# Fewer, longer attention stretches between the dense matmuls of a retention and feed-forward kernel

## The chip, the core and the metric

The kernel runs on one core of a Trainium2 chip. Its engines are TensorE (PE, matrix products; PEld is its weight load), VectorE (DVE), ScalarE (ACT), GpSimd (POOL) and SyncE (SP, which here only issues transfers). Each works through its own queue in program order and waits for the others by semaphores. PE writes its results to PSUM, where the kernel's tiles take eight banks; everything else lies in SBUF. The metric is the device time of one launch in microseconds, lower is better.

## What is computed

Causal retention over 8 batches, 8 heads, 576 tokens, head size 64, and then a feed-forward layer with a snake-like activation:

```python
scores = scale * np.matmul(q, k.transpose(0, 1, 3, 2))
Dmat = np.where(rel >= 0, gamma[:, None, None] ** rel[None, :, :], 0.0)
attn = np.matmul(scores * Dmat[None, :, :, :], v)
x = np.ascontiguousarray(attn.transpose(0, 2, 1, 3)).reshape(B * S, H * D)   # 4608 x 512
h = x @ w_in                       # 512 -> 2048
s = np.sin(alpha * h)
g = h + s * s / (alpha + 1e-09)
out = g @ w_out                    # 2048 -> 512
```

## The kernel before

**Tiling.** The 4608 rows of `x` are nine blocks of 512. Block `b` (0 to 7) holds the first 512 tokens of batch `b`; block 8 holds the last 64 tokens of all eight batches. The decay factors are folded into the casts of `q` and `k` to 16 bit, so a score needs only a causal mask (0 or 1). The first 512 tokens of a batch are two halves `p` of 256 tokens, and each half is two chunks `g` of 128. Inside a chunk scores are masked and multiplied with `v`; what earlier chunks contribute comes through a state: `outer` computes `kv` per chunk, `chain` on POOL fades and adds it up (lines 353 to 360), and `states` multiplies it with `q`.

**Steps of one batch** (class `Attention`):
- `cast_half`: half of the heads of `k` or `q` of one `p`, multiplied with the factors (128x512), on DVE for batches 5 to 7. Four of them per `p`, eight per batch.
- `crossed(p)`: two transposes by DMA, `kT` and `qT`, issued by SP.
- `scores(p, y)`: 64x64 matmuls for two of four pairs of heads, `a = 2y` and `2y + 1`, into one tile `sc` of two PSUM banks, and a DVE instruction that multiplies the mask in and writes `ret` in 16 bit. In batches 4 to 7 (`split(b)`) keys of a chunk come as an early half (`r = 0`), which all 128 tokens of the chunk may see, and a late half (`r = 1`), which only the last 64 tokens may see; so each `sc` holds, for each `a`, 128 columns and 64 columns, 192 of 256 used (lines 366 to 399).
- `outer((0, 1))`: 64 matmuls of 64x64 into `kv`, then ACT copies `kv` to `kvs`, and POOL's chain follows.
- `values(p)`: 64x64 matmuls of `ret` and `v` into `o`; `states(p)`: 128x128 matmuls into the same `o` (4 for `p = 0`, 8 for `p = 1`); `take_x(p)`: copies `o` to `x` in 16 bit. `add_states` is `states` and `take_x` on ACT.

The last 64 tokens of four batches at a time are class `Rest`: `scores` (32 matmuls of 64x64, a mask on DVE) and `values` (32 of 64x64, 16 of 128x64 with the states, two copies by ACT).

**Order.** It is written out by hand. A table (lines 588 to 928) covers the start and blocks 0 and 1; it isn't changed. Then a loop over blocks `n = 2 ... 8` runs 16 units `u` each: `gemm1(n, u)` (four matmuls of 128x512 into a bank `hps`, and the sine on ACT), then whatever `at_unit(u, ...)` has put there, then the square on ACT, the product on DVE (`gT`, line 560) and a quarter of `gemm2` of the block before (four matmuls of 128x512). Every fourth quarter ends a PSUM tile `ops`, which ACT copies out and SP sends. In units 1, 5, 9 and 13 the quarter comes before the square and the product.

While block `n` is computed, attention runs for batch `n + 1` (`A`), and batch `n + 2` is cast and transposed (`A2`); its raw `q` and `k` were loaded from unit 12 of the block before. `CASTS[n]` names the units of the eight casts. `crossed(0)` follows one unit after the fourth, `crossed(1)` one after the eighth. So PE switches from dense matmuls to attention and back in units 0, 2, 7 and 10 of each block 3 to 6. In block 5 it does so also in units 12 and 14, for `Rest` of batches 0 to 3; `Rest` of batches 4 to 7 stands in units 0 and 2 of block 7.

**Buffers.** PSUM: tag "mm" is two tiles of two banks (for `sc`, `kv`, `o`), "hp" three banks (for `hps`), "op" one bank (`ops`). SBUF: `ret` has 4 buffers, `kT` and `qT` 3, `v` 6, raw loads 6, `osb` 4.

Of the kernel before, what the change touches and what calls it, by code (L numbers as in the profile page):

```python
# [9 lines left out]
F32 = mybir.dt.float32  # L10
F16 = mybir.dt.float16
ADD = mybir.AluOpType.add
MULT = mybir.AluOpType.mult
# [3 lines left out]
def kernel(  # L17
# [10 lines left out]
    nc = tc.nc  # L28
# [4 lines left out]
    P = 128  # L33
# [44 lines left out]
    work = ctx.enter_context(tc.tile_pool(name="w", bufs=1))  # L78
    psum = ctx.enter_context(tc.tile_pool(name="p", bufs=1, space=bass.MemoryType.PSUM))
# [6 lines left out]
    two = const.tile([P, 192], F16, tag="two", bufs=1)  # L86
# [23 lines left out]
    half = {}  # L110

    def split(b):
        return b >= 4
# [7 lines left out]
    def load_v(b, p):  # L121
        t_ = work.tile([P, H, 2, D], F16, tag="v16", bufs=6, name="v16")
        half[b, "v", p] = t_
        if split(b):
            for g, s, xs in pieces(b, p):
                nc.gpsimd.dma_start(t_[halves(g), :, s], v[b, :, xs, :].rearrange("h i d -> i h d"))  # L126
            return None
        i_ = nc.gpsimd.dma_start(
            t_.rearrange("p h r d -> p h (r d)"),
            v[b, :, 256 * p : 256 * p + 256, :].rearrange("h (i r) d -> i h (r d)", r=2),  # L130
        )
        half[b, "v", p] = t_
        return i_

    def load_rest_v(G):
        t_ = work.tile([P, 2 * H, D], F16, tag="vr16", bufs=1, name="v16")
        for e in range(2):
            b = 4 * G + 2 * e
            nc.gpsimd.dma_start(t_[halves(e)], v[b : b + 2, :, 512:576, :].rearrange("b h i d -> i (b h) d"))
        half[G, "v", "rest"] = t_  # L140

    def load(b, nm, p):
        t_ = work.tile([P, H, 2 * D], F32, tag="raw", bufs=6, name=nm + "32")
        raw[b, nm, p] = t_
        if split(b) and nm == "k":
            for g, s, xs in pieces(b, p):
                nc.sync.dma_start(
                    t_[halves(g), :, 64 * s : 64 * s + 64], src[nm][b, :, xs, :].rearrange("h i d -> i h d")
                )
            return None  # L150
        return nc.sync.dma_start(t_, src[nm][b, :, 256 * p : 256 * p + 256, :].rearrange("h (i r) d -> i h (r d)", r=2))
# [13 lines left out]
    def load_rest(G, nm):  # L165
        t_ = work.tile([P, H, 2 * D], F32, tag="raw", bufs=6, name=nm + "32")
        for e in range(2):
            b = 4 * G + 2 * e
            nc.sync.dma_start(
                t_[halves(e)].rearrange("p h (x d) -> p (h x) d", d=D),  # L170
                src[nm][b : b + 2, :, 512:576, :].rearrange("b h i d -> i (b h) d"),
            )
        raw[G, nm, "rest"] = t_
# [29 lines left out]
    def cast_half(b, nm, p, t, eng):  # L203
        if (b, nm, p) not in half:
            half[b, nm, p] = work.tile([P, 4, 2, 2, D], F16, tag=nm + "16", bufs=nbuf[nm], name=nm + "16")
        if eng is nc.scalar:
            for y in range(4):
                for r in range(2):
                    h = head_of(y, t)
                    eng.mul(  # L210
                        half[b, nm, p][:, y, r, t, :], raw[b, nm, p][:, h, D * r : D * r + D],
                        fac[nm][:, 2 * h + r : 2 * h + r + 1],
                    )
            return
        eng.tensor_tensor(  # L215
            half[b, nm, p][:, :, :, t, :],
            raw[b, nm, p].rearrange("p (a t) (r d) -> p a t r d", t=2, r=2)[:, :, t],
            (ct if nm == "k" and split(b) else fac[nm]).rearrange("p (a t r) -> p a t r", a=4, t=2)[:, :, t].unsqueeze(3).to_broadcast([P, 4, 2, D]),
            MULT,
        )  # L220

    def halves(n):
        return slice(64 * n, 64 * n + 64)

    def head_of(a, t):
        return 2 * a + t
# [17 lines left out]
    class Attention:  # L244
# [144 lines left out]
        def scores_mask(self, p, y):  # L389
            sc = self.sc.pop((p, y))  # L390
            ret = work.tile([P, 2, 512], F16, tag="ret", bufs=4, name="ret")
            n, m_ = (192, two) if split(self.b) else (256, mask[:, 0:256])
            nc.vector.tensor_tensor(  # L393
                ret.rearrange("p t (z x) -> p (t z) x", z=2)[:, :, 0:n],
                sc.rearrange("p t (z x) -> p (t z) x", z=2)[:, :, 0:n],
                m_.unsqueeze(1).to_broadcast([P, 4, n]),
                MULT,
            )
            self.ret[p, y] = ret

        def new_o(self, p, *tags):
            if tags:
                o = [psum.tile([P, 512], F32, tag=t, bufs=3 if t == "hp" else 1, name="o") for t in tags]
            else:
                o = psum.tile([P, 2, 512], F32, tag="mm", bufs=2, name="o")
                o = [o[:, 0], o[:, 1], o]
            self.o[p] = o, set()
# [118 lines left out]
    def gemm1(n, fc, o=None):  # L526
        gemm1_pe(n, fc, o)
        sine(n, fc)
# [403 lines left out]
    V, A_, G_ = nc.vector, nc.scalar, nc.gpsimd  # L932

    with tc.manual_schedule():
# [34 lines left out]
        def of(b):  # L969
            if b not in att:  # L970
                att[b] = Attention(b)
            return att[b]
# [130 lines left out]
        rest = [Rest(0), Rest(1)]  # L1103
        nc.sync.dma_start(two, two_dram.ap())
        nc.sync.dma_start(ct, ct_dram.ap())
        for p, nm in HALVES:
            load(4, nm, p)
        CASTS = (), (), (5, 5, 6, 6, 7, 8, 9, 9), (4, 5, 6, 6, 8, 9, 10, 10), *[(1, 3, 4, 5, 6, 8, 9, 10)] * 2
        for n in range(2, NBLK):
            A = A2  # L1110
            todo = {}

            def at_unit(u, *fs):
                todo.setdefault(u, []).extend(fs)

            if A:
                if n == 2:
                    at_unit(1, lambda: A.scores(0, 0), lambda: A.scores(0, 1))
                    at_unit(4, lambda: A.outer((0, 1)), lambda: A.chain((0, 1, 2, 3)), lambda: A.scores(1, 0))
                else:  # L1120
                    at_unit(0, lambda: A.scores(0, 0), lambda: A.scores(0, 1))
                    at_unit(2, lambda: A.outer((0, 1)), lambda: A.chain((0, 1, 2, 3)), lambda: A.scores(1, 0))
                at_unit(7, lambda: A.scores(1, 1), lambda: A.values(0), lambda: A.add_states(0))
                at_unit(10, lambda: A.values(1), lambda: A.add_states(1))
            bn = n + 2
            if bn < B:
                A2 = of(bn)
                at_unit(0, lambda: load_v(bn, 0), lambda: load_v(bn, 1))
                for i, u in enumerate(CASTS[n]):
                    p, nm, t = i // 4, "kq"[i // 2 % 2], i % 2  # L1130
                    at_unit(u, lambda p=p, nm=nm, t=t: cast_half(bn, nm, p, t, V if n > 2 else G_))
                at_unit(CASTS[n][3] + 1, lambda: A2.crossed(0))
                at_unit(CASTS[n][7] + 1, lambda: A2.crossed(1))
            else:
                A2 = None
            if bn + 1 < B:
                for i, (p, nm) in enumerate(HALVES):
                    at_unit(i + 12, lambda nm=nm, p=p: load(bn + 1, nm, p))
            if n in (3, 5):
                at_unit(15, *[lambda nm=nm: load_rest((n - 3) // 2, nm) for nm in "kq"])  # L1140
                at_unit(15, lambda: load_rest_v((n - 3) // 2))
            R = rest[(n - 4) // 2] if n in (4, 6) else None
            if n in (4, 6):
                at_unit(11 if n == 4 else 5, lambda: cast((n - 4) // 2, "k", "rest", V))
                at_unit(13 if n == 4 else 8, lambda: cast((n - 4) // 2, "q", "rest", V), lambda: R.crossed())
            if n in (5, 7):
                at_unit(12 if n == 5 else 0, lambda: rest[n // 6].scores())
                at_unit(14 if n == 5 else 2, lambda: rest[n // 6].values())
            for u in range(16):
                gemm1(n, u)  # L1150
                for f in todo.get(u, []):
                    f()
                last = second[0][1] % 4 == 3
                if not last:
                    square(n, u, A_)
                    product(n, u)
                next_second()
                if last:
                    square(n, u, A_)
                    product(n, u)  # L1160
        while second:
            next_second()
        for z in range(2):
            cols = slice(256 * z, 256 * z + 256)
            o = psum.tile([P, 512], F32, tag="hp", bufs=3, name="ops")
            for fk in range(FC):
                nc.tensor.matmul(  # L1167
                    o[:, 0:256], gT[NBLK - 1][:, fk, 3 * P : 4 * P], w_out16[:, fk, cols],
                    start=(fk == 0), stop=(fk == FC - 1),
# [35 lines left out]
```

## Time and profile before

| | |
|---|---|
| median of three runs | 313.4 us (312.19 to 314.8) |
| profiled execution | 313.51 us, of which the span (first to last instruction) is 311.7 us |
| mean granted TensorE clock | 0.984 |
| busy, share of the span | PE 96%, ACT 73%, DVE 61%, POOL 44% |
| instructions on PE | 3145 matmuls |
| moved by DMA | 44.74 MB |

Times in the profile's views are microseconds from the span's start. A row of the timeline or of the groups reads: line, engine, operation, output<-inputs, shapes, count. Matmuls are pipelined and their ends are modelled, so PE's cost is better read from starts, or from the chain of work that ended last, in which each piece ends where the next begins. In an `L` number `L535` is the first product (`gemm1`), `L574` the second (`gemm2`), `L376` scores, `L312` `kv`, `L413` values, `L439` states, `L482`, `L500` and `L508` the same for the last tokens, `L393` and `L487` the masks, `L215` the casts.

### The profile page before, as it was taken

How to read it: one execution, taken by the hardware profiler on the slowest of the kernel's cores; microseconds unless marked ns; L12 is line 12 of the kernel's file. 1: busy time of each engine (PE TensorE's matmuls, PEld its weight loads, DVE VectorE, ACT ScalarE, POOL GpSimd, SP SyncE). 2: the span in 40 equal slices, each digit the busy share in tenths (PEclk: the TensorE clock that was granted, in tenths of full speed). 3: DMA queues.
4: the chain of work that ended last, by engine and by line, in shares of the span. 5: the costliest groups of instructions: out<-in, count | busy, mean ns of one | idle time of the engine just before them, and what ended most of it. 6: DMA issues, size and time to landing. Idle time of an engine off the chain costs nothing.

```text
span 311.7 us, 7656 instructions
## 1 busy us (share of the span) xinstructions
PE 298.4 (96%) x3145; PEld 152.6 (49%) x3145; DVE 189.6 (61%) x267; ACT 228.5 (73%) x374; POOL 136.2 (44%) x158
## 2 busy tenths in 40 slices
PE   5799989899999999999999999999999999999994
PEld 5586444444444444444544444444444444444443
DVE  2688857799655357956886788654846343444401
ACT  1479861699588878887888788778887888888710
POOL 4778655669969956940692065025600000000000
PEclk9579999999999999999999999999999999999999
DMA  8999999996999899999999985698331111122133
GB/s 219 202 179 186 274 174 283 205 229 134 153 171 241 162 171 210 178 166 226 195 163 193 161 216 125 103 116 124 69 67 37 35 36 34 34 54 49 34 67 68
DMA packets 118018, 44.74 MB, mean 144 GB/s; under 512 B 84432, under 2 KB 113504, under 8 KB 117984
## 3 DMA queue, kind: packets, MB, share of 16 engines
q1 hardware_dynamic: 83792, 35.08, 57.1%
q0 software_dynamic: 33600, 8.92, 29.5%
q8 instruction: 24, 0.39, 0.5%
q10 hardware_dynamic: 592, 0.28, 0.4%
q14 instruction: 10, 0.08, 0.1%
HBM read 36.91 MB, written 9.44 MB: 149 GB/s over the span
## 4 chain that ended last, share of the span: by engine, by line
PE 80%; DVE 8%; DMA 4%; POOL 3%; ACT 2%; issue 1%; SPq 1%; DVEq 0%; POOLq 0%; ACTq 0%
PE ops L574 36%; PE hps L535 32%; PE sc L376 2%; DVE ret L393 2%; DMA qT<-q 2%; DMA k<-in_k_dram 2%; DVE gT L560 2%; PE o L413 2%; PE o L439 2%; PE hps L1016 2%; PE kv L312 1%; PE tr L275 1%; PE ops L1167 1%; DVE gT L1043 1%; DVE kvs L334 1%; POOL w_in L104 1%
## 5 line engine op out<-in xcount | busy, mean ns | idle before, releaser
L560 DVE SCALAR_TENSOR_TENSOR gT<-ss_t,inva,hps 128x512 f16<-128x512 f16 x136 | 100.6, 745 | 87.3 <-ACT ss_t L553 86.5
L574 PE MATMUL ops<-w_out,gT 128*128 128x512 f16 x560 | 140.8, 379 | 0.0
L535 PE MATMUL hps<-x,w_in 128*128 128x512 f16 x480 | 120.9, 379 | 1.0 <-DVE gT L560 0.7
L544 ACT ACTIVATE s_t<-hps,alpha_t 128x512 f16<-128x512 f32 x136 | 92.9, 685 | 32.8 <-PE hps L535 31.6
L535 PEld LDWEIGHTS <-w_in 128*128 128x128 f16 x544 | 52.9, 98 | 64.6 <-issue 1.7
L574 PEld LDWEIGHTS <-gT 128*128 128x128 f16 x560 | 52.7, 98 | 60.0 <-DVE gT L560 0.3
L553 ACT ACTIVATE ss_t<-s_t 128x512 f16<-128x512 f16 x127 | 79.9, 631 | 2.5
L346 POOL TENSOR_TENSOR s<-kvs,cn 128x512 f16<-128x512 f32 x28 | 30.9, 1103 | 55.7 <-ACT kvs L319 46.5
L584 ACT COPY osb<-ops 128x512 f32<-128x512 f32 x31 | 18.2, 586 | 13.2 <-PE ops L574 12.8
L126 POOL DMA_DIRECT2D v<-in_v_dram x32 | 22.0, 732 | 0.0
L215 DVE TENSOR_TENSOR q<-q,cn 128x512 f16<-128x512 f32 x18 | 16.5, 923 | 3.8 <-DMA q<-in_q_dram 3.8
L393 DVE TENSOR_TENSOR ret<-sc,mask 128x1024 f16<-128x1024 f32 x12 | 14.4, 1215 | 5.9 <-PE sc L376 5.9
L236 ACT CAST x<-o 128x1024 f16<-128x1024 f32 (+1 forms) x17 | 14.9, 889 | 3.8 <-PE o L439 3.5
L535 PE MATMUL hps<-x_rest,w_in 128*128 128x512 f16 x64 | 16.4, 379 | 0.0
L215 POOL TENSOR_TENSOR q<-q,cn 128x512 f16<-128x512 f32 x14 | 14.9, 1078 | 0.1
L393 DVE TENSOR_TENSOR ret<-sc,two 128x768 f16<-128x768 f32 x16 | 14.9, 951 | 0.0
L555 POOL TENSOR_TENSOR ss_t<-s_t 128x512 f16<-128x512 f16 x10 | 10.5, 1059 | 6.6 <-ACT s_t L544 4.0
L376 PE MATMUL sc<-qT,kT 64*64 64x128 f16 (+1 forms) x512 | 11.7, 225 | 0.9 <-DMA qT<-q 0.5
L359 POOL TENSOR_TENSOR kvs<-s,kvs 128x256 f32<-128x256 f32 x15 | 11.9, 791 | 1.2
L376 PEld LDWEIGHTS <-kT 64*64 64x64 f16 x512 | 8.6, 114 | 7.4 <-issue 5.1
L358 POOL TENSOR_TENSOR s<-kvs,cn 128x256 f32<-128x256 f32 x15 | 11.9, 792 | 0.0
L413 PE MATMUL o<-ret,v 64*64 64x128 f16 (+1 forms) x512 | 10.6, 218 | 0.1
(69 smaller groups left out, 202.7 us busy)
## 6 DMA issues: line engine op xcount, KB each, us to landing
out_dram<-osb SPq DMA_DIRECT2D x70, 128.0 KB, 3.2
q<-in_q_dram SPq DMA_DIRECT2D x14, 512.0 KB, 6.7
k<-in_k_dram SPq DMA_DIRECT2D x32, 128.0 KB, 5.1
k<-in_k_dram SPq DMA_DIRECT2D x7, 512.0 KB, 7.0
q<-in_q_dram SPq DMA_DIRECT2D x8, 256.0 KB, 4.7
v<-in_v_dram POOLq DMA_DIRECT2D x8, 256.0 KB, 6.1
w_in<-in_moe_w_in_dram POOLq DMA_DIRECT2D x4, 512.0 KB, 7.7
w_out<-in_moe_w_out_dram POOLq DMA_DIRECT2D x4, 512.0 KB, 8.4
```

Source lines behind the costliest of these rows:

```text
L126: nc.gpsimd.dma_start(t_[halves(g), :, s], v[b, :, xs, :].rearrange("h i d -> i h d"))
L215: eng.tensor_tensor(half[b, nm, p][:, :, :, t, :], raw[b, nm, p].rearrange("p (a t) (r d) -> p a t r d", t=2, r=2)[:, :, t], (ct if nm == ...
L346: (eng or nc.gpsimd).tensor_tensor(d_, self.kvs[:, n].unsqueeze(2).to_broadcast([P, 4, 2, D]), g2.unsqueeze(3).to_broadcast([P, 4, 2, D]), ...
L376: nc.tensor.matmul(sc[halves(g), t, x : x + 128 - 64 * late], T[0][halves(t), 2 * a + r, halves(g)], T[1][halves(t), 2 * a : 2 * a + 2, 64 ...
L393: nc.vector.tensor_tensor(ret.rearrange("p t (z x) -> p (t z) x", z=2)[:, :, 0:n], sc.rearrange("p t (z x) -> p (t z) x", z=2)[:, :, 0:n], ...
L413: nc.tensor.matmul(o[g][halves(t), x0 : x0 + 128].rearrange("p (r i) -> p r i", r=2)[:, :, i0:], x, y, start=(t, g) not in begun, stop=las ...
L535: nc.tensor.matmul(hps, w_in16[:, a, fc * P : (fc + 1) * P], x_of[n][:, a], start=(a == 0), stop=(a == KT - 1),)
L544: nc.scalar.activation(s_t, hps, mybir.ActivationFunctionType.Sin, bias=0.0, scale=alpha_t[:, fc : fc + 1],)
L553: nc.scalar.activation(ss_t, s_t, mybir.ActivationFunctionType.Square)
L560: nc.vector.scalar_tensor_tensor(gT[n][:, fc, :], ss_t, inva[:, fc : fc + 1], hps, MULT, ADD)
L574: nc.tensor.matmul(ops[n, c], gT[n][:, fk, c * P : (c + 1) * P], w_out16[:, fk, :], start=(fk == 0), stop=(fk == FC - 1),)
L584: nc.scalar.copy(osb, ops.pop((n, c)))
```

## The change

It concerns batches 4 to 7, that is blocks 3 to 6.

- Scores go into three tiles and not four: `near(p)` holds the early halves of all four pairs of heads of one `p` (4 x 128 columns), `late` the late halves of both `p` (8 x 64 columns). Three masks of 128x1024 take the place of four of 128x768. `all_values(p)` does the work of `values(p)`, all early halves first and then all late ones. The matmuls are the same in number and shape.
- The steps stand in units 0, 4 and 8. Unit 0: `near(0)`, its mask, `outer`, `chain`. Unit 4: `near(1)`, `late`, the first one's mask; the second's is queued in unit 5. Unit 8: `all_values(0)`, `all_values(1)`, both `states`, and the copies to `x`, the first on ACT, the second on DVE.
- In block 5 values of `p = 1` stand in unit 11, and the last tokens' scores and values are put between the batch's own steps in units 8 and 11.
- The casts move: see `CASTS`. In block 2 nothing moves.
- By the order of the queues: on POOL the eight loads of `v` that a block issues now stand behind the chain of that block and not ahead of it; on SP the transposes move with the casts.

```diff
+        def near(self, p):
+            sc = psum.tile([P, 2, 512], F32, tag="mm", bufs=2, name="sc")
+            T = self.T[p]
+            for a in range(4):
+                for t in range(2):
+                    for g in range(2):
+                        nc.tensor.matmul(
+                            sc[halves(g), t, 128 * a : 128 * a + 128],
+                            T[0][halves(t), 2 * a, halves(g)], T[1][halves(t), 2 * a : 2 * a + 2, halves(g)],
+                            start=(a == 0), stop=(a == 3), skip_group_check=True,
+                        )
+            self.sc[p] = sc
+
+        def late(self):
+            sc = psum.tile([P, 2, 512], F32, tag="mm", bufs=2, name="sc")
+            for j in range(8):
+                p, a = divmod(j, 4)
+                T = self.T[p]
+                for t in range(2):
+                    for g in range(2):
+                        nc.tensor.matmul(
+                            sc[halves(g), t, 64 * j : 64 * j + 64], T[0][halves(t), 2 * a + 1, halves(g)],
+                            T[1][halves(t), 2 * a : 2 * a + 2, 64 * g + 32 : 64 * g + 64],
+                            start=(j == 0), stop=(j == 7), skip_group_check=True,
+                        )
+            self.sc["late"] = sc
+
+        def masked(self, name):
+            sc = self.sc.pop(name)
+            n, m_ = (8, two[:, 128:192]) if name == "late" else (4, two[:, 0:128])
+            ret = work.tile([P, 2, 512], F16, tag="ret", bufs=4, name="ret")
+            nc.vector.tensor_tensor(
+                ret.rearrange("p t (a x) -> p (t a) x", a=n), sc.rearrange("p t (a x) -> p (t a) x", a=n),
+                m_.unsqueeze(1).to_broadcast([P, 2 * n, 512 // n]), MULT,
+            )
+            self.ret[name] = ret
+
+        def all_values(self, p):
+            for r in range(2):
+                for a in range(4):
+                    for t in range(2):
+                        for g in range(2):
+                            x0, m = (256 * p + 64 * a, 64) if r else (128 * a, 128)
+                            self.into_o(
+                                p, t, g, 128 * a, 32 * r,
+                                half[self.b, "v", p][halves(g), head_of(a, t), r, :],
+                                self.ret["late" if r else p][halves(g), t, x0 : x0 + m],
+                            )
...
-        CASTS = (), (), (5, 5, 6, 6, 7, 8, 9, 9), (4, 5, 6, 6, 8, 9, 10, 10), *[(1, 3, 4, 5, 6, 8, 9, 10)] * 2
+        CASTS = (), (), (5, 5, 6, 6, 7, 8, 9, 9), (4, 6, 6, 7, 7, 8, 9, 9), *[(1, 2, 3, 3, 6, 7, 9, 9)] * 2
...
                 if n == 2:
                     at_unit(1, lambda: A.scores(0, 0), lambda: A.scores(0, 1))
                     at_unit(4, lambda: A.outer((0, 1)), lambda: A.chain((0, 1, 2, 3)), lambda: A.scores(1, 0))
+                    at_unit(7, lambda: A.scores(1, 1), lambda: A.values(0), lambda: A.add_states(0))
+                    at_unit(10, lambda: A.values(1), lambda: A.add_states(1))
                 else:
-                    at_unit(0, lambda: A.scores(0, 0), lambda: A.scores(0, 1))
-                    at_unit(2, lambda: A.outer((0, 1)), lambda: A.chain((0, 1, 2, 3)), lambda: A.scores(1, 0))
-                at_unit(7, lambda: A.scores(1, 1), lambda: A.values(0), lambda: A.add_states(0))
-                at_unit(10, lambda: A.values(1), lambda: A.add_states(1))
+                    at_unit(0, lambda: A.near(0), lambda: A.masked(0))
+                    at_unit(0, lambda: A.outer((0, 1)), lambda: A.chain((0, 1, 2, 3)))
+                    at_unit(4, lambda: A.near(1), A.late, lambda: A.masked(1))
+                    at_unit(5, lambda: A.masked("late"))
+                    if n == 5:
+                        at_unit(8, lambda: A.all_values(0), rest[0].scores, lambda: A.add_states(0))
+                        at_unit(11, lambda: A.all_values(1), rest[0].values, lambda: A.states(1, last=True))
+                        at_unit(11, lambda: A.take_x(1, V))
+                    else:
+                        at_unit(8, lambda: A.all_values(0), lambda: A.all_values(1))
+                        at_unit(8, lambda: A.states(0, last=True), lambda: A.states(1, last=True))
+                        at_unit(8, lambda: A.take_x(0, A_), lambda: A.take_x(1, V))
...
-            if n in (5, 7):
-                at_unit(12 if n == 5 else 0, lambda: rest[n // 6].scores())
-                at_unit(14 if n == 5 else 2, lambda: rest[n // 6].values())
+            if n == 7:
+                at_unit(0, lambda: rest[1].scores())
+                at_unit(2, lambda: rest[1].values())
```

## The prediction

> **What bounds the kernel now.** I read the page's head and the shares of its chain first (the chain is the work that ended last, followed back), then who TensorE (PE) waited for, then busy time by block. A block is one value of `n`: 16 steps, called units, each with one `gemm1` of four matmuls and one `gemm2` of four.
>
> ```profile
> span 311.7 us, 7656 instructions
> ...
> PE 80%; DVE 8%; DMA 4%; POOL 3%; ACT 2%; issue 1%; SPq 1%; DVEq 0%; POOLq 0%; ACTq 0%
> ```
>
> The next line is from the list of waits (us in total, times, longest), the two after it from the windows of blocks 4 and 5 (length, then busy time and count of PE, PE's weight loads, DVE, ACT, POOL, then granted clock, DMA share, GB/s).
>
> ```profile
> PE hps L535 <- DVE gT L560: 0.7, 3, 0.3
> ```
>
> ```profile
> 143.50:174.75 31.25, 31.25 (x334) 15.12 (x332) 24.18 (x32) 25.32 (x40) 15.05 (x18) 1.00 1.29 191
> 174.75:207.37 32.62, 32.62 (x413) 16.01 (x412) 22.80 (x29) 26.19 (x42) 11.33 (x12) 1.00 0.74 138
> ```
>
> PE is the bound: it never stops in these blocks, at the full granted clock, while DVE is busy 24.18 of 31.25 us and ACT 25.32. PE's waits for DVE come to 0.7 us in the whole program. So an edit here is worth exactly the PE time it takes out, unless it makes another engine late.
>
> What attention costs PE is read from the chain, where only PE stands in these blocks (start, us, what). First block 4, then the two stretches of the last tokens in block 5:
>
> ```profile
> 144.37 0.47 PE sc L376 x32
> 144.84 0.97 PE ops L574 x4
> ...
> 148.40 0.64 PE kv L312 x64
> 149.04 0.29 PE sc L376 x9
> 149.33 0.97 PE ops L574 x4
> ...
> 158.07 0.30 PE sc L376 x16
> 158.37 0.35 PE o L413 x32
> 158.72 0.33 PE o L439 x4
> 159.05 0.86 PE ops L574 x4
> ...
> 164.23 0.47 PE o L413 x32
> 164.70 0.55 PE o L439 x8
> 165.25 0.86 PE ops L574 x4
> ```
>
> ```profile
> 199.90 0.38 PE sc L482 x32
> 200.27 0.97 PE ops L574 x4
> ...
> 203.83 0.38 PE o L500 x32
> 204.21 0.57 PE o L508 x16
> ```
>
> A unit is 2 x 0.86 = 1.73 us. A stretch costs the time between the dense groups, plus 0.11 where the next dense group shows 0.97 and not 0.86. So the four stretches of block 4 cost 0.58, 1.04, 0.98 and 1.02, together 3.62, and 32 x 0.8636 + 3.62 = 31.26 is the block. The two of the last tokens cost 0.48 and 0.95.
>
> **The sum on PE.** The matmuls of attention are the same before and after: per batch 64 for scores (half of them 128 columns wide, half 64), 64 for `kv`, 64 for values, 12 with states. What the change removes is a stretch's fixed part, F, the cost of going from 128x128 matmuls to 64x64 ones and back. The rows give it: write w for 32 score matmuls, which are as wide as 32 value matmuls, and s for one state matmul.
> - F + w = 0.58 (first stretch)
> - F + w + 8s = 1.02 (fourth), so 8s = 0.44
> - F + 1.5w + 4s = 0.98 (third), so w/2 = 0.98 - 0.58 - 0.22 = 0.18
>
> Hence w = 0.36 and F = 0.22. It checks in block 5: 0.48 - 0.22 = 0.26 for 32 matmuls of 64 columns, which is below w, as it should be.
>
> After the change blocks 3, 4 and 6 have three stretches for four: saved 3 x 0.22. Block 5 has four (units 0, 4, 8, 11) for six (0, 2, 7, 10, 12, 14), since the last tokens' scores and values now stand between 64x64 matmuls of the batch: saved 2 x 0.22. Together 5 x 0.22 = 1.1 us. The order inside a stretch changes too (all 128-column ones, then all 64-column ones, instead of alternating); from 0.26 per 32 narrow ones, 32 wide ones cost 2 x 0.36 - 0.26 = 0.46, so the sums agree and I take nothing for it. Bounds: the F of single stretches is rounded to 0.02 or so, and the second stretch leaves 1.04 - 0.22 - 0.18 = 0.64 for `kv`, where 64 narrow matmuls at 0.26 per 32 would take 0.52; if that 0.12 is a cost of `kv` and scores meeting in this order, it might go too, 4 x 0.12. So the gain on PE is 0.9 to 1.6, taken at 1.1.
>
> **DVE, where the cover is thin.** It does three masks of 128x1024 for four of 128x768, and one copy of `x` that was ACT's. The nearest rows (busy, mean ns of one):
>
> ```profile
> L487 DVE TENSOR_TENSOR ret<-sc,mask 128x1024 f16<-128x1024 f32 x2 | 2.5, 1225 | 0.0
> L237 DVE CAST x<-o 128x512 f16<-128x512 f32 x3 | 2.0, 686 | 0.0
> ```
>
> A 128x1024 copy was never made on DVE; it lies between 0.69 and 2 x 0.69, and I take 1.2, by the mask row, which also reads PSUM. ACT loses 1 us per block and is not the bound. More important is the order. In blocks 4 and 5 the casts move to units 1, 2, 3, 3, 6, 7, 9, 9, so both casts of the first `q` stand in unit 3, and the masks follow in units 4 and 5. Behind them waits the product (L560), which frees one of three `hps` banks: product u must end before `gemm1` u+3 starts. The rows (DVE's timeline, then POOL's):
>
> ```profile
> 151.55 1.01 DVE L215 TENSOR_TENSOR k<-k,ct 128x512 f16<-128x512 f32 x1
> ...
> 153.25 1.57 DVE L215 TENSOR_TENSOR q<-q,cn 128x512 f16<-128x512 f32 x1
> 154.74 0.73 DVE L560 SCALAR_TENSOR_TENSOR gT<-ss_t,inva,hps 128x512 f16<-128x512 f16 x1
> 155.40 1.24 DVE L215 TENSOR_TENSOR q<-q,cn 128x512 f16<-128x512 f32 x1
> ...
> 162.86 0.68 DVE L215 TENSOR_TENSOR q<-q,cn 128x512 f16<-128x512 f32 x1
> ```
>
> ```profile
> 150.40 1.04 POOL L346 TENSOR_TENSOR s<-kvs,cn 128x512 f16<-128x512 f32 x1 [14.30 <-ACT kvs L319]
> ...
> 153.23 1.04 POOL L346 TENSOR_TENSOR s<-kvs,cn 128x512 f16<-128x512 f32 x1
> ...
> 160.43 5.50 POOL L126 DMA_DIRECT2D v<-in_v_dram  x8
> ```
>
> A `q` cast takes 0.68 when POOL computes nothing, and 1.24 to 1.57 while POOL runs the state chain (150.40 to 160.43). The one at 153.25 began just after a POOL instruction and ended 0.55 us after that one's end: it stood still meanwhile. The change starts this chain at unit 0, not 2, so the four casts of units 1 to 3 now all lie under it. The Trainium skill, page "SBUF — State Buffer", section "Who interferes with whom", says that a DVE instruction with two SBUF inputs and a GpSimd one that reads SBUF contend, and whoever comes second is blocked for the whole of the other. The trace agrees, with those 0.55 us; this rule speaks against the change.
>
> Worked out from the start of `gemm1` in unit 3, t = 0: a cast and a product (1.01 + 0.73) about fill a unit, so product 2 ends by about 1.9. Two casts take 1.4 (2 x 0.68) to 3.1 (2 x 1.57), so product 3 ends at 4.0 to 5.8; `gemm1` 6 starts at 3 x 1.73 + 0.7 (the new stretch of unit 4: 0.22 + 0.26 + 0.23) = 5.9. A mask and a product, 1.97, make product 4 end at 6.0 to 7.8, against 7.6, and product 5 at 8.0 to 9.7, against 9.3. With the pair that the trace has (1.57 + 1.24) product 5 is at 9.4, but DVE's rows overlap by some 0.08 each (153.25 + 1.57 is past 154.74), and over six instructions that is 0.5 earlier. So PE loses 0 to 0.4 us per block in blocks 4 and 5; I take 0, with half a microsecond of cover. Block 3 has such pairs in units 6 and 7, ahead of the long stretch of unit 8, which delays `gemm1` 9 by 1.6; block 6 has only the last tokens' casts.
>
> **What else moves, at no cost.**
> - POOL: the loads of `v` for a later batch were issued ahead of the chain and now stand behind it. In block 4 the chain would run from about 146.5 to 156.6, the eight issues take 5.5 more, and `v` lands at most 6.8 later (row below), by 169; it is wanted in block 5's unit 0, past 175. Cover 6 us.
> - SP: the transposes of `kT` and `qT` are issued up to two units earlier and read in units 0 and 4 (before 0 and 2): more time, not less. Output transfers queue behind them as before.
> - PSUM: `late` needs the bank that ACT's copy of `kv` frees in unit 0; four units are ample. `all_values` needs both score banks, whose masks end by unit 6.
> - New wait on DVE in unit 8: the copy of `x` waits for that stretch's end. Product 8 is behind it, done some 0.9 + 1.6 + 0.2 + 1.2 + 0.75 = 4.6 us after `gemm1` 8 began, wanted at 5.2 + 1.6.
>
> The landing of `v` is from the view of that tile, 100 to 205 us:
>
> ```profile
> DMA to landing us min/median/max: 3.2/4.7/6.8
> ```
>
> The profiled execution took 313.5 us, its span 311.7 and 1.8 around it; the median of the three runs is 313.4, with 312.19 to 314.8. I take the sum from the median: 313.4 - 1.1 = 312.3.
>
> **Rivals.**
> - DVE late, so slower than before. Place: units 3 to 5 of blocks 4 and 5. If each cast of unit 3 waits for two POOL instructions and not for one, it takes about 1.57 + 0.9 = 2.5; product 3 then ends at 1.9 + 5.0 + 0.75 - 0.5 (the overlap) = 7.2, which is 1.3 late, and product 5, with the 0.4 that the two masks add, 1.7 late. Two blocks give 3.4, so 313.4 - 1.1 + 3.4 = 315.7. It turns into a loss where each block loses over 0.55, which is where the pair takes over some 3.7 us. For it: all four casts are now under the chain. Against: no cast in a row above takes over 1.57. This is what the rule of the Trainium skill's page above would do at its worst.
> - DVE a little late: the upper end of my sum, 0.8 in two blocks, 313.1.
> - F isn't saved: the 0.22 belongs to the kinds of matmul and not to the stretch, so nothing is gained, 313.4. Against: three stretches with different contents give the same F.
> - `kv` and scores meet better, and the gain is 1.6: 311.8.
>
> **Chances.** Forecast 0.68, DVE a little late 0.10, DVE late 0.07, F not saved 0.07, larger gain 0.08. The four that lie between 311.8 and 313.4 hold 0.93; runs of one kernel scatter by about 1.3 us either way, their median by less, so the range is 310.9 to 313.8. Over 1% (3.1 us, about what a measurement of this kernel can tell from no change): no case gains that much by itself; scatter and what I have not seen get 0.07. Slower by over 1% is past 316.5: the worst DVE case and a little more, 0.06. Within: 0.87.
>
> **What would show it.** In the changed kernel's chain blocks 3 to 6 are PE alone, block 4 takes 31.0 us (31.25 now) and block 5 32.2 (32.62), and stretches cost about 1.04, 0.7 and 1.6. The wait of `hps` for `gT` stays under 1 us. Wrong would be: that wait at several us, in units 6 to 8 of blocks 4 and 5, with casts of unit 3 past 1.6 us; PE waiting for `v`, `kT` or `qT` in unit 0 or 4; or blocks that keep their length without any wait.

## The result, and the profile after

Over 22 runs each, the kernel before took 313.41 us in the median and the changed one 311.64 us (310.86 to 313.0). The ratio is 0.9946, with a 95% interval of 0.9934 to 0.9958: a gain of 1.7 us, between 1.3 and 2.1. The forecast was 312.3, a gain of 1.1. Its sign and its mechanism hold; the gain that it gave is too small by 0.2 to 1.0 us.

The head of the page after, the shares of the chain of work that ended last, and PE's wait for a free `hps` bank from the list of waits:

```profile
span 309.8 us, 7642 instructions
...
PE 80%; DVE 8%; DMA 4%; POOL 3%; ACT 2%; issue 1%; SPq 1%; DVEq 0%; POOLq 0%; ACTq 0%
```

```profile
PE hps L584 <- DVE gT L609: 0.7, 3, 0.3
```

Nothing has taken PE's place: the shares are the same, and the wait that the edit could have lengthened is 0.7 us as before. The lines have new numbers: L584 is `gemm1`, L623 `gemm2`, L407 `near`, L421 `late`, L462 values, L488 states. The windows of blocks 4 and 5 (length, busy time of PE, PE's weight loads, DVE, ACT, POOL, granted clock, DMA share, GB/s):

```profile
143.04:173.97 30.93, 30.93 (x333) 15.11 (x332) 25.27 (x32) 24.39 (x39) 15.04 (x18) 1.00 1.27 187
173.97:206.12 32.15, 32.15 (x413) 16.11 (x412) 24.15 (x29) 25.36 (x41) 16.68 (x20) 1.00 1.13 168
```

Block 4 went from 31.25 to 30.93, block 5 from 32.62 to 32.15, both at the full granted clock and both filled by PE. DVE gained 1.1 us of work in block 4 (24.18 to 25.27) and ACT lost 0.9, mostly the copy of `x` that moved. The chain inside block 4 shows the three stretches (start, us, what):

```profile
143.90 0.35 PE sc L407 x16
144.25 0.55 PE kv L312 x64
144.79 0.97 PE ops L623 x4
...
151.81 0.35 PE sc L407 x16
152.15 0.25 PE sc L421 x32
152.41 0.97 PE ops L623 x4
...
159.42 0.82 PE o L462 x64
160.24 0.78 PE o L488 x12
161.02 0.86 PE ops L623 x4
```

Read as before, with 0.11 added where the next dense group shows 0.97, they cost 1.00, 0.71 and 1.60 us, together 3.31, where four cost 3.62.

By the starts of `gemm1` in the traces, blocks 3 to 6 became shorter by 0.30, 0.32, 0.47 and 0.26, together 1.35 us. The two profiled executions differ by 1.9 in span. The other 0.6 lies outside the edited blocks: block 3's `gemm1` began 0.17 earlier (112.27 against 112.10 in the chains), and the stretch from the last copy to the end was 3.8 us for 4.2. Both vary as much between the kernels below, in which nothing there differs: among the nine traces the first is anywhere in 1.4 us, the second either 3.7 to 3.8 or 4.2 to 4.3. So 1.35 us is what the trace gives to the edit, and it lies inside the interval of the measured gain.

### The profile page after: what moved, and what is told of

Same layout as the page of the kernel before. It is cut to its first block, busy times and chain, and to the rows that moved or that the text cites. A ratio compares the mean times of both kernels' runs of the same rounds, so it can differ in the third digit from the quotient of the medians.

```text
span 309.8 us, 7642 instructions
## 1 busy us (share of the span) xinstructions
PE 296.7 (96%) x3145; PEld 152.7 (49%) x3145; DVE 192.2 (62%) x267; ACT 224.9 (73%) x370; POOL 133.8 (43%) x158
## 4 chain that ended last, share of the span: by engine, by line
PE 80%; DVE 8%; DMA 4%; POOL 3%; ACT 2%; issue 1%; SPq 1%; DVEq 0%; POOLq 0%; ACTq 0%
PE ops L623 37%; PE hps L584 32%; DMA qT<-q 2%; DVE ret L393 2%; DMA k<-in_k_dram 2%; DVE gT L609 2%; PE o L462 2%; PE o L488 2%; PE hps L1065 2%; PE sc L376 1%; PE kv L312 1%; PE ops L1226 1%; PE tr L275 1%; PE sc L407 1%; DVE gT L1092 1%; DVE kvs L334 1%
## 5 line engine op out<-in xcount | busy, mean ns | idle before, releaser
L623 PE MATMUL ops<-w_out,gT 128*128 128x512 f16 x560 | 140.8, 379 | 0.0
L584 PE MATMUL hps<-x,w_in 128*128 128x512 f16 x480 | 120.9, 379 | 1.0 <-DVE gT L609 0.7
L584 PEld LDWEIGHTS <-w_in 128*128 128x128 f16 x544 | 52.8, 98 | 64.6 <-issue 1.6
L623 PEld LDWEIGHTS <-gT 128*128 128x128 f16 x560 | 53.0, 98 | 60.9 <-DVE gT L609 0.3
L346 POOL TENSOR_TENSOR s<-kvs,cn 128x512 f16<-128x512 f32 x28 | 30.2, 1078 | 60.0 <-ACT kvs L319 50.9
L215 DVE TENSOR_TENSOR q<-q,cn 128x512 f16<-128x512 f32 x18 | 15.4, 880 | 4.2 <-DMA q<-in_q_dram 4.2
L584 PE MATMUL hps<-x_rest,w_in 128*128 128x512 f16 x64 | 16.4, 379 | 0.0
L432 DVE TENSOR_TENSOR ret<-sc,two 128x1024 f16<-128x1024 f32 x12 | 14.6, 1218 | 0.0
L236 ACT CAST x<-o 128x1024 f16<-128x1024 f32 (+1 forms) x13 | 10.8, 851 | 3.7 <-PE o L488 3.4
L358 POOL TENSOR_TENSOR s<-kvs,cn 128x256 f32<-128x256 f32 x15 | 11.0, 730 | 0.0
L215 POOL TENSOR_TENSOR k<-k,cn 128x512 f16<-128x512 f32 x9 | 9.9, 1109 | 0.8 <-DMA k<-in_k_dram 0.7
L462 PE MATMUL o<-ret,v 64*64 64x128 f16 (+1 forms) x512 | 10.1, 218 | 0.1
L462 PEld LDWEIGHTS <-v 64*64 64x64 f16 x512 | 7.6, 110 | 4.8 <-issue 4.3
```

The lines of the kernel that those rows point to most:

```text
L215: eng.tensor_tensor(half[b, nm, p][:, :, :, t, :], raw[b, nm, p].rearrange("p (a t) (r d) -> p a t r d", t=2, r=2)[:, :, t], (ct if nm == ...
L346: (eng or nc.gpsimd).tensor_tensor(d_, self.kvs[:, n].unsqueeze(2).to_broadcast([P, 4, 2, D]), g2.unsqueeze(3).to_broadcast([P, 4, 2, D]), ...
L432: nc.vector.tensor_tensor(ret.rearrange("p t (a x) -> p (t a) x", a=n), sc.rearrange("p t (a x) -> p (t a) x", a=n), m_.unsqueeze(1).to_br ...
L462: nc.tensor.matmul(o[g][halves(t), x0 : x0 + 128].rearrange("p (r i) -> p r i", r=2)[:, :, i0:], x, y, start=(t, g) not in begun, stop=las ...
L584: nc.tensor.matmul(hps, w_in16[:, a, fc * P : (fc + 1) * P], x_of[n][:, a], start=(a == 0), stop=(a == KT - 1),)
L623: nc.tensor.matmul(ops[n, c], gT[n][:, fk, c * P : (c + 1) * P], w_out16[:, fk, :], start=(fk == 0), stop=(fk == FC - 1),)
```

## The experiments

All are variants of the changed kernel. Lengths of blocks are taken from start to start of `gemm1`; ratios are to the kernel before.

| kernel | ratio (95%) | blocks 3, 4, 5, 6 (us) | block 7 |
|---|---|---|---|
| before | 1 | 31.23, 31.25, 32.62, 31.19 | 29.06 |
| changed | 0.9946 (0.9934 to 0.9958) | 30.93, 30.93, 32.15, 30.93 | 29.06 |
| unit 8 in two | 0.9978 (0.9955 to 1.0001) | 31.16, 31.22, 32.24, 31.16 | 29.06 |
| last tokens apart | 0.9960 (0.9937 to 0.9982) | 30.93, 30.93, 32.36, 31.07 | 29.06 |
| packed, old stretches | 0.9994 (0.9973 to 1.0015) | 31.17, 31.13, 32.64, 31.13 | 29.06 |
| `kv` first | 0.9959 (0.9934 to 0.9983) | 30.97, 30.97, 32.19, 30.97 | 29.06 |
| old casts | 0.9959 (0.9941 to 0.9977) | 30.93, 30.98, 32.15, 30.93 | 29.06 |
| more casts | 1.0016 (0.9997 to 1.0034) | 30.93, 31.53, 34.00, 30.93 | 29.06 |
| last tokens in block 6 | 0.9949 (0.9931 to 0.9967) | 31.02, 30.93, 32.25, 32.15 | 27.63 |

The intervals are some 0.6 us either way, so most of what follows is read from the blocks.

**One stretch more per block.**

```diff
-                        at_unit(8, lambda: A.all_values(0), lambda: A.all_values(1))
-                        at_unit(8, lambda: A.states(0, last=True), lambda: A.states(1, last=True))
-                        at_unit(8, lambda: A.take_x(0, A_), lambda: A.take_x(1, V))
+                        at_unit(8, lambda: A.all_values(0), lambda: A.states(0, last=True))
+                        at_unit(8, lambda: A.take_x(0, A_))
+                        at_unit(10, lambda: A.all_values(1), lambda: A.states(1, last=True))
+                        at_unit(10, lambda: A.take_x(1, V))
```

> The changed kernel, but in blocks 3, 4 and 6 the stretch of unit 8 is cut in two: values and states of p = 0 in unit 8, those of p = 1 in unit 10. Tiles, masks and matmuls stay. Theory (what is saved is the fixed cost F of a stretch, 0.22 us): the two stretches cost 0.80 and 1.02 where the one cost 1.60, so the blocks take 31.15 us and not 30.93, and the kernel about 312.3 us, 0.7 over the changed one. Rival (the gain is in the packing of the scores and in the fewer masks): blocks stay at 30.93, the kernel at 311.6.

The chain of this kernel in block 6:

```profile
223.27 0.47 PE o L462 x32
223.74 0.33 PE o L488 x4
224.07 0.86 PE ops L623 x4
...
227.53 0.47 PE o L462 x32
228.00 0.55 PE o L488 x8
228.55 0.86 PE ops L623 x4
```

The two stretches cost 0.80 and 1.02, 0.22 over the 1.60 of the one, and blocks 3 and 6 take 31.16 as expected. Block 4 has 0.06 more on top, and block 5, which the edit doesn't touch, 0.09; both sit in unit 0, where `kv` stands (see the last section). The time rose by 0.0032 of 313.4, or 1.0 us, 0.7 being expected. The theory of the stretch holds; that the whole gain lies in the packing doesn't.

**The last tokens by themselves again.**

```diff
-                    if n == 5:
-                        at_unit(8, lambda: A.all_values(0), rest[0].scores, lambda: A.add_states(0))
-                        at_unit(11, lambda: A.all_values(1), rest[0].values, lambda: A.states(1, last=True))
-                        at_unit(11, lambda: A.take_x(1, V))
...
+            if n in (5, 7):
+                at_unit(12 if n == 5 else 0, lambda: rest[n // 6].scores())
+                at_unit(14 if n == 5 else 2, lambda: rest[n // 6].values())
```

> The changed kernel, but in block 5 the last tokens' scores and values stand by themselves in units 12 and 14 again, as before, and block 5 is otherwise like blocks 3, 4 and 6. Theory: five stretches in block 5 where the changed kernel has four, and six before: 0.22 us back, block 5 takes 32.15 + 0.22 = 32.37, the kernel 311.9. Rival (joining the last tokens to others is worth nothing, their cost is their own matmuls): block 5 stays at 32.15 or falls, since the others are in three stretches.

Block 5 takes 32.36, 0.21 over the changed kernel and 0.01 from what was expected: five stretches for four. (Block 6 has 0.14 more than in the changed kernel, though nothing differs there; the last section comes back to it.) So joining the last tokens to a batch saves stretches too, at the same price.

**Packing without fewer stretches.**

```diff
+                    at_unit(0, lambda: A.near(0), A.late, lambda: A.masked(0), lambda: A.masked("late"))
+                    at_unit(2, lambda: A.outer((0, 1)), lambda: A.chain((0, 1, 2, 3)))
+                    at_unit(2, lambda: A.near(1), lambda: A.masked(1))
+                    at_unit(7, lambda: A.all_values(0), lambda: A.add_states(0))
+                    at_unit(10, lambda: A.all_values(1), lambda: A.add_states(1))
```

(with the last tokens apart and the casts at their old units)

> Packing alone: scores in three tiles with three masks as in the changed kernel, but four stretches per block (units 0, 2, 7, 10), six in block 5, the casts at their old units and both copies of x on ACT. Theory (stretches): the four cost 0.71, 1.00 to 1.09, 0.80 and 1.02, so a block takes 31.15 to 31.25 us, and the kernel 313.0 to 313.4, as before. Rival (packing): 311.6 to 312, blocks at 30.9.

Its blocks are within 0.12 us of those before, 0.06 to 0.12 shorter in blocks 3, 4 and 6, and 0.02 longer in block 5; the ratio of 0.9994 can't be told from 1. Three score tiles, three masks and a new order inside the stretches, taken alone, take 0.22 us off the four blocks together (126.29 to 126.07). From here to the changed kernel (124.94) it is 1.13, and between the two stand the five stretches fewer, at 0.226 each; the casts and one copy of `x` also differ, but PE waits for nothing in these blocks in either kernel. So the packing alone is a sixth of the 1.35, and the figure is soft, since single blocks vary by up to 0.14 at `kv` (last section). What else the packing is good for is argued from the buffers and wasn't run: six tiles per batch (three of scores, `kv`, two of `o`) go through a PSUM tag that holds two at a time in three visits, seven need four.

**`kv` ahead of the scores.**

```diff
-                    at_unit(0, lambda: A.near(0), lambda: A.masked(0))
                     at_unit(0, lambda: A.outer((0, 1)), lambda: A.chain((0, 1, 2, 3)))
+                    at_unit(0, lambda: A.near(0), lambda: A.masked(0))
```

> The changed kernel, but in unit 0 the matmuls of kv come ahead of the scores, as they did in unit 2 before. The changed kernel saved 0.31 us in a block where F alone is 0.22; its first stretch took 1.00, which leaves 0.55 for kv, where the old order left 0.64. Theory (kv and scores meet worse in the old order): the first stretch takes 1.04 to 1.09, blocks 30.97 to 31.02, the kernel 311.8 to 312.0. Rival (the order is worth nothing, and the 0.09 is something else): 1.00 and 311.6.

The chain in block 4, to be held against 0.35 and 0.55 in the changed kernel:

```profile
144.77 0.64 PE kv L312 x64
145.41 0.29 PE sc L407 x16
145.70 0.97 PE ops L623 x4
```

The first stretch costs 1.04 in all four blocks, and each is 0.04 longer, as the theory said. But it isn't settled by that: the packed kernel with old stretches also has `kv` first and `near` behind it in unit 2, and there the same pair costs 1.01, 0.97, 1.05 and 0.97 in the four blocks, on average no more than the 1.00 of scores first.

**Casts at their old units.**

```diff
-        CASTS = (), (), (5, 5, 6, 6, 7, 8, 9, 9), (4, 6, 6, 7, 7, 8, 9, 9), *[(1, 2, 3, 3, 6, 7, 9, 9)] * 2
+        CASTS = (), (), (5, 5, 6, 6, 7, 8, 9, 9), (4, 5, 6, 6, 8, 9, 10, 10), *[(1, 3, 4, 5, 6, 8, 9, 10)] * 2
```

> The changed kernel with the casts at their old units (4, 5, 6, 6, 8, 9, 10, 10 in block 3; 1, 3, 4, 5, 6, 8, 9, 10 in blocks 4 and 5). In units 4 and 5 DVE then has a mask, a q cast and a product each. Worked out from the start of gemm1 in unit 3, product 3 ends at 3.0, product 4 at about 6.4 (wanted at 7.6) and product 5 at 9.0 to 9.3 (wanted at 9.3). Theory (PE alone sets the time while DVE keeps its cover): 311.6 to 312.2 us, PE's wait for gT up by 0 to 0.3 in each of blocks 4 and 5. Rival (the move of the casts carries part of the gain): over 312.5, with PE waiting for gT.

Blocks are as in the changed kernel (30.98 for 30.93 in block 4 is the largest difference), and PE waits for nothing between 110 and 250 us. Moving the casts, which puts two `q` casts into one unit, was neither needed nor harmful.

**More casts in unit 3.** One in block 4 and two in block 5, of which nothing is used:

```diff
+        def extra(b):
+            nc.vector.tensor_tensor(
+                work.tile([P, 4, 2, D], F16, tag="extra", bufs=1, name="extra"),
+                raw[b, "q", 0].rearrange("p (a t) (r d) -> p a t r d", t=2, r=2)[:, :, 1],
+                fac["q"].rearrange("p (a t r) -> p a t r", a=4, t=2)[:, :, 1].unsqueeze(3).to_broadcast([P, 4, 2, D]),
+                MULT,
+            )
...
+                for _ in range(max(0, n - 3)):
+                    at_unit(3, lambda: extra(bn))
```

> The changed kernel with casts of q added in unit 3, whose result nobody reads: one more in block 4, two more in block 5. In the changed kernel the pair took 2.69 us there and product 5 ended 0.64 us before gemm1 of unit 8 wanted its bank. Theory (the cover is 0.6 us, and past it PE loses one for one): at 1.35 a cast, block 4 grows by 0.7 us and block 5 by 2.1, PE waits for gT in units 6 to 8, the kernel takes 314.4. Rival (cover is far larger, since later units have idle time on DVE): both blocks keep their length, 311.6.

First the margin in the changed kernel, from DVE's timeline in block 4 and then PE's (starts of the first matmul of each `gemm1`):

```profile
151.00 2.69 DVE L215 TENSOR_TENSOR q<-q,cn 128x512 f16<-128x512 f32 x2
153.61 0.73 DVE L609 SCALAR_TENSOR_TENSOR gT<-ss_t,inva,hps 128x512 f16<-128x512 f16 x1
154.27 1.21 DVE L432 TENSOR_TENSOR ret<-sc,two 128x1024 f16<-128x1024 f32 x1
155.40 0.73 DVE L609 SCALAR_TENSOR_TENSOR gT<-ss_t,inva,hps 128x512 f16<-128x512 f16 x1
156.06 1.21 DVE L432 TENSOR_TENSOR ret<-sc,two 128x1024 f16<-128x1024 f32 x1
157.19 0.73 DVE L609 SCALAR_TENSOR_TENSOR gT<-ss_t,inva,hps 128x512 f16<-128x512 f16 x1
```

```profile
154.94 1.03 PE L584 MATMUL hps<-x,w_in 128*128 128x512 f16 x4
...
156.67 1.03 PE L584 MATMUL hps<-x,w_in 128*128 128x512 f16 x4
...
158.39 1.03 PE L584 MATMUL hps<-x,w_in 128*128 128x512 f16 x4
```

The three products are those of units 3, 4 and 5, the three `gemm1` those of units 6, 7 and 8, which want their banks. Product 3 ends at 154.34, 0.60 ahead of its taker; product 4 at 156.13, 0.54 ahead; product 5 at 157.92, 0.47 ahead. Each mask and product takes DVE 1.79 from one product's end to the next, more than a unit, so the margin shrinks until unit 6. (The 0.64 of the expectation took the start of `gemm1` 8 from the chain, 158.56, where a piece begins only when the one before it ends.) Now DVE with two casts more, in block 5, and PE's waits between 110 and 250 us (us in total, times, longest): one of 0.3 in block 4 and one of 1.6 in block 5.

```profile
182.03 2.69 DVE L215 TENSOR_TENSOR q<-q,cn 128x512 f16<-128x512 f32 x2
184.65 2.23 DVE L1158 TENSOR_TENSOR extra<-q,cn 128x512 f16<-128x512 f32 x2
186.80 0.73 DVE L609 SCALAR_TENSOR_TENSOR gT<-ss_t,inva,hps 128x512 f16<-128x512 f16 x1
187.46 1.21 DVE L432 TENSOR_TENSOR ret<-sc,two 128x1024 f16<-128x1024 f32 x1
```

```profile
PE hps L584 <- DVE gT L609: 1.9, 2, 1.6
```

Block 4 grew by 0.60 and block 5 by 1.85, where 0.7 and 2.1 were expected: the added casts took DVE 1.10 and 2.23 us, not 1.35 each. Less the margin of 0.47 that is 0.63 and 1.76. So beyond half a microsecond PE loses one for one, and the idle time that DVE has in later units doesn't help. The kernel lands at 313.93 us, no longer faster than before.

**The other last tokens joined as well.** The loads of the last `k` and `q` of batches 4 to 7 move from unit 15 to unit 5 of block 5, their casts and transposes from block 6 to units 12 and 14 of block 5, their scores and values from block 7 to block 6:

```diff
-                    if n == 5:
+                    if n in (5, 6):
...
-            if n == 7:
-                at_unit(0, lambda: rest[1].scores())
-                at_unit(2, lambda: rest[1].values())
...
-                at_unit(15, *[lambda nm=nm: load_rest((n - 3) // 2, nm) for nm in "kq"])
+                at_unit(15 if n == 3 else 5, *[lambda nm=nm: load_rest((n - 3) // 2, nm) for nm in "kq"])
...
-                at_unit(11 if n == 4 else 5, lambda: cast((n - 4) // 2, "k", "rest", V))
-                at_unit(13 if n == 4 else 8, lambda: cast((n - 4) // 2, "q", "rest", V), lambda: R.crossed())
+                at_unit(11 if n == 4 else 12, lambda: cast(n - 4, "k", "rest", V))
+                at_unit(13 if n == 4 else 14, lambda: cast(n - 4, "q", "rest", V), lambda: R.crossed())
```

(with `R` set for `n` in 4 and 5, and `rest[n - 5]` in units 8 and 11)

> One step on: the last tokens of batches 4 to 7 too are joined to a batch, in block 6 as in block 5; their loads are issued from unit 5 of block 5, their casts in units 12 and 14. Block 7 then has no stretch. One stretch fewer in sum (block 6 four for three, block 7 none for two). Theory: blocks 6 and 7 together 0.22 us shorter than in the changed kernel, the kernel at 311.4. Rival (the earlier loads, casts and transposes make something late in blocks 5 and 6): PE waits there for qT, v or gT, 311.6 or more.

Blocks 6 and 7 take 32.15 + 27.63 = 59.78 us, where the changed kernel takes 30.93 + 29.06 = 59.99: 0.21 less, as expected, and PE waits for nothing there. In the time it can't be seen (0.9949 against 0.9946), since 0.2 us is a third of the interval, and in this trace unit 0 of blocks 3 and 5 lost 0.09 and 0.10 to pauses at `kv`. It is faster than the kernel before, and not shown to be faster than the changed one.

## Why the forecast held, step by step

- *PE is the bound, so the edit is worth the PE time it takes out.* Right. Every block's length is the sum of its matmuls and stretches in all traces, except where casts were added and for the pauses at `kv` (last section).
- *F = 0.22 per stretch, five stretches fewer.* Right. Worked out of three equations then, it was measured four ways now: 0.22 where a stretch was cut in two, 0.21 where the last tokens left the others, 0.21 where the second group joined, and 1.13 for five between the packed kernel with old stretches and the changed one. The Trainium skill, page "TensorEngine Tiling (Array Packing)", section "Key Properties", says that a change of the tiling mode drains TensorE; it gives no price. These runs give one for the whole way to 64x64 matmuls and back, about 0.22 us, and don't show how much of it is a drain. The trace does show that the loading of weights, which otherwise runs under the matmuls (15.11 us of it in the 30.93 of block 4), breaks off there. The list of waits of the changed kernel has it idle for 0.4 us ahead of seven of the eight stretches that begin with `near`, with no wait named (us in total, times, longest):

```profile
PEld L407 <- issue: 3.0, 7, 0.4
```

- *Costs of the new stretches, 1.04, 0.7 and 1.6; block 4 at 31.0, block 5 at 32.2.* Measured 1.00, 0.71 and 1.60; 30.93 and 32.15.
- *The order inside a stretch, taken at nothing, with up to 0.12 per block kept for `kv` and scores meeting better.* This is the term that was too small. Blocks 3 to 6 saved 1.35, which is 5 x 0.22 and 0.25 more, or 0.06 per block. It lies in the stretch with `kv`, as the bound had it: in block 4 that stretch cost 1.04 with 16 scores, half of them narrow, and costs 1.00 now with 16 wide ones; at 0.18 and 0.23 for these scores and 0.22 for F, `kv` has 0.64 and 0.55 of it. It came with the packing: the kernel that is packed and keeps the old stretches already has 0.22 of it, with `kv` still ahead of the scores. Why is open. The order of `kv` and scores alone isn't shown to be the cause, since the two kernels with `kv` first disagree, and which scores stand beside `kv` was not varied by itself. By the blocks the gain of 1.35 ended halfway between the forecast and the rival of a larger gain (1.6, 311.8); by the median, 311.64, that rival, which had a chance of 0.08, came closer than the forecast.
- *DVE: the two casts of unit 3 take 1.4 to 3.1; half a microsecond of cover.* Right, and closely: 2.69, and 0.47 left at the tightest place. The copy of `x`, taken at 1.2, takes 1224 ns. The rule of the Trainium skill's page "SBUF — State Buffer" (section "Who interferes with whom") that spoke against the change was at work, with 2.69 for a pair that takes 2 x 0.68 without POOL, but within the cover. The rival in which DVE makes the kernel slower is real, as the added casts show; it begins 0.5 us further on.
- *POOL's loads of `v` behind the chain, by 169 at the latest, wanted past 175.* Right: in block 4 they were issued from 156.03, where 156.6 was worked out, and PE waits for no `v`. They took up to 8.5 us to land, not 6.8, so by about 170; the cover of 6 us was about 5:

```profile
156.03 5.49 POOL L126 DMA_DIRECT2D v<-in_v_dram  x8
```

- *F isn't saved.* Fell: blocks go up by 0.21 to 0.23 with each stretch that is put back.

## What to carry to other kernels

When PE is full, look at how often it changes between large and small tile shapes and not only at what the small matmuls take: the change has a fixed price, which can be solved from a few stretches with different contents before anything is edited. Packing results more densely into PSUM may be worth little by itself and still be what allows two visits to become one. Before lengthening the queue of an engine with idle time, compute the margin at its tightest unit: an engine busy for 25 of 31 us had half a microsecond to give.

## What the runs showed that was not expected

The stretch with `kv` isn't constant. With scores first it costs 1.00 us in most blocks, but 1.05 and 1.09 in two blocks of the kernel with unit 8 in two, 1.05 in one block with the old casts, 1.14 in one block with the last tokens apart and 1.09 twice in the last kernel, which is 6 blocks of 24, always through a longer time for the 64 matmuls of `kv`, with PE waiting for no one. The chain of the kernel with the last tokens apart shows it in block 6, where the other blocks have 0.55:

```profile
207.21 0.35 PE sc L407 x16
207.56 0.69 PE kv L312 x64
```

Each of these matmuls is as narrow as any in the kernel, and there are more in a row than elsewhere. The trace's records of single matmuls show the four longer pauses as one gap each: two `kv` matmuls late in the row start 0.08 to 0.13 us apart, where their neighbours start 0.008 apart, and the weight loads stop with them. What makes the pause wasn't found, and no run here was made to find it.
